# A two-layer ReLU²/cosine network behind linear attention: 1024 tokens take half of their directly computed weight blocks as a third seven-product slot

## The chip, the cores and the metric

One core of a Trainium2 chip runs the whole program. The metric is the device time of one execution in microseconds. In the traces PE is the matrix engine (TensorE), PEld its loading of weights, DVE VectorE, ACT ScalarE, POOL GpSimd, SP SyncE; SP and POOL issue the DMAs, each from a queue that it works through in order.

## The reference

Linear attention with a norm, then two layers of the same shape; 4608 tokens, 512 wide, 2048 hidden. The layers' weights come as 64-bit floats, the rest as 32-bit.

```
kv  = einsum('bhsd,bhse->bhde', k, v)
out = einsum('bhsd,bhde->bhse', q, kv);  x = out / rms(out) * g_norm   # as 4608 x 512
h = x @ w_in;   x = relu(h)**2 @ w_out                                   # first layer
h = x @ w_in2;  out = (h * cos(h)) @ w_out2                              # second layer
```

## The kernel before

**Numbers.** Each 32-bit operand is split into a high half of reduced width and a low half, the rest (`h` on ACT, `l` on DVE), and a product is three matmuls: high-high, high-low, low-high. The 64-bit weights are taken apart into words and made into 32-bit floats on DVE and ACT (`words` L107, `value` L121).

**Stage one** (`run_chunks` L815) works in chunks (t, f): token tile t (nine of 512 tokens) and weight block f. A weight block is 128 of the 2048 hidden columns; the first layer's 16 blocks are shared out, 0 to 7 to stage one (`NH` = 8), 8 to 15 to the slots. A chunk is `layer_in` (12 matmuls of 512 columns into one bank, L374), `act_relu2` (relu, square, halves, L388) and, two chunks later, `layer_out` (12 matmuls into four accumulators, L411). After a tile's last block `evict` (L401) writes the accumulators to `p_d`. Attention runs in between, in the first 49 chunks (`nAtt`). After chunk 49 the square is DVE's work (L396), before it ACT's (L394). There are 72 chunks.

**The slots** (`run_slots` L843) are for the other half of the first layer and for the whole second layer. A slot (m, t, q) is layer m, a tile of 2 x ht tokens (`TILES` L56, ht 512 or 384) and a group q of 4 weight blocks; every product of two 2 x 2 block matrices is made of seven block products instead of eight. A slot has 84 matmuls of ht columns for the first product (`first_product` L499, banks FA and FB) and, in the first layer, 84 of ht columns for the second (`second_product` L629, banks SA and SB); in the second layer the second product's matmuls are 256 columns wide. Combinations of blocks are needed on both sides: `x_block` (L456) makes those of the inputs for a tile's first slot, `s_block` (L590) those of the hidden values (a subtraction for four of the seven, a high half on ACT at L618, a low half on DVE at L619), `add` (L531) and `keep` sum the first product, `drain_product` (L657) adds the second product to the tile's sums (L670). A tile's last slot writes the sums to `y_d`, from which the second layer reads. The first layer has 5 tiles x 2 groups = 10 slots, the second 5 x 4 = 20. First products run ahead of second ones by 1.25 slots (`LAG2`), so PE's time from the first slot's start to slot position 1.25 holds first products only; from there both alternate matmul by matmul.

**Conversion of weights for the slots.** `load_w` (L129) brings a block pair, `conv_steps` (L165) turns it into seven combinations and their halves (four sums or differences at L175, a high half on ACT at L192, a low half on DVE at L194 in two parts of 3 and 4 blocks) and writes them to `wi_d` (first product's weights) or `ws_d` (second product's); `load_wi` and `load_ws` (L485, L490) read them back, 512 KB for each block product. Kinds "pair" and "seven" (512 wide) run in stage one from `w_stream`; kind "pairs" (1024 wide) runs in the slots from `late_stream` (L740), 7 items, for the second layer's first product. Its buffer for the raw words is single (`bufs=1` in `run_slots`' pools), so a load waits until the item before has been stored.

**What sets the order.** Everything that isn't a matmul is a job with a position, in chunks or, after `nA0`, in slots; jobs are sorted by it and emitted between matmuls, and a scheduler then fixes each engine's order, which the engine works through in order. Two lines place what the change touches:

```
w_stream.place(w_at, 0.5, range(2 * NH - NRAW, 2 * NH - NRAW + 2))
late_stream.place([pos(n) for n in (0.95, 2.5, 3.25, 4.5, 6.4, 8.3, 11.3)], 0, lead=0.5)
```

An item of `late_stream` at position n is converted in six steps from n to n + 0.4; the next one is loaded 0.5 ahead of its own position, but not before n + 0.62.

## Time and profile before

| what | value |
|---|---|
| median of 3 runs | 1561.06 us (1559.02 to 1561.68) |
| the profiled execution | 1560.63 us |
| its span | 1558.8 us |
| busy, share of the span | PE 98%, DVE 83%, ACT 69%, POOL 7% |
| TensorE clock granted | full in every slice of the page |
| HBM traffic | 427 MB, 274 GB/s |
| stage one | to 494.86 us |
| the slots | from 494.86 us |

Part 2 of the page cuts the span into 40 slices of 39 us: the first two are the ones in which PE has idle time, and DVE's digits are highest in stage one's second half and in the first slots. Part 4 (the chain that ended last) is PE for 87%. Windows give an engine's busy time for a stretch; a wait is the idle time of an engine before an instruction, put down to what came last.

### The profile page before, as it was taken

To read this page: it belongs to the slowest core of one execution; us is meant where nothing else is said; L and a number is where in the kernel's file an instruction comes from. 1 tells how busy PE (TensorE), PEld (TensorE's weight loads), DVE (VectorE), ACT (ScalarE), POOL (GpSimd) and SP (SyncE) were. 2 spreads that over 40 slices of the span, in tenths; PEclk is the share of its full clock that TensorE was granted. 3 is DMA by queue.
4 is the path that set the end of the run, shared out by engine and by line. 5 is a ranking of instruction groups with operands and counts; after the bars stand their busy time and mean duration, and the time that the engine had idled before them with its cause. 6 is when DMAs were issued, how large, how long until landed. Compare 5 with 4: busy or idle time off the path is not lost.

```text
span 1558.8 us, 24668 instructions
## 1 busy us (share of the span) xinstructions
PE 1533.3 (98%) x9104; PEld 1345.9 (86%) x9104; DVE 1294.2 (83%) x1743; ACT 1077.1 (69%) x1529; POOL 109.8 (7%) x173
## 2 busy tenths in 40 slices
...
GB/s 337 270 149 244 276 283 275 222 214 214 206 226 298 325 253 367 299 380 267 364 339 372 265 281 255 249 285 215 254 247 284 215 247 273 298 326 292 301 311 171
DMA packets 222295, 426.71 MB, mean 274 GB/s; under 512 B 18016, under 2 KB 138080, under 8 KB 222176
## 3 DMA queue, kind: packets, MB, share of 16 engines
...
q10 hardware_dynamic: 160, 0.00, 0.0%
HBM read 317.72 MB, written 81.79 MB: 256 GB/s over the span
## 4 chain that ended last, share of the span: by engine, by line
PE 87%; DVE 5%; DMA 3%; ACT 2%; issue 2%; SPq 0%; POOL 0%; DVEq 0%; ACTq 0%; POOLq 0%
PE FB L509 16%; PE FA L509 16%; PE SA L642 16%; PE SB L642 15%; PE acc L420 11%; PE l L383 9%; PE o L383 1%; PE ss L383 1%; DMA xraw<-x_d 1%; DMA sum<-part 1%; PE o L259 1%; DMA ws_d<-raw 1%; DMA kvld<-in_kv 1%; DVE gl L619 1%; PE l L259 1%
## 5 line engine op out<-in xcount | busy, mean ns | idle before, releaser
L509 PE MATMUL FB<-xh,wi 128*128 128x512 f32 (+1 forms) x840 | 301.4, 370 | 0.0
L509 PE MATMUL FA<-xh,wi 128*128 128x512 f32 (+1 forms) x840 | 301.4, 370 | 0.0
L642 PE MATMUL SB<-ws,gh 128*128 128x256 f32 x1008 | 233.0, 280 | 0.6 <-ACT part L667 0.6
L642 PE MATMUL SA<-ws,gh 128*128 128x256 f32 x1008 | 233.2, 280 | 0.0
L642 PEld LDWEIGHTS SA<-ws,gh 128*128 128x128 f32 x1008 | 183.7, 188 | 12.8 <-issue 0.5
L642 PEld LDWEIGHTS SB<-ws,gh 128*128 128x128 f32 x1008 | 183.3, 188 | 12.6 <-ACT part L667 0.8
L509 PEld LDWEIGHTS FB<-xh,wi 128*128 128x128 f32 x840 | 157.2, 188 | 9.6
L509 PEld LDWEIGHTS FA<-xh,wi 128*128 128x128 f32 x840 | 157.1, 188 | 9.0
L642 PE MATMUL SB<-ws,gl 128*128 128x256 f32 x504 | 141.2, 280 | 0.3 <-DVE gl L619 0.3
L642 PE MATMUL SA<-ws,gl 128*128 128x256 f32 x504 | 141.2, 280 | 0.1
L619 DVE TENSOR_TENSOR gl<-y,gh 128x1024 fp32r<-128x1024 f32 (+1 forms) x98 | 109.5, 1118 | 36.7 <-ACT gh L618 36.7
L668 POOL DMA_DIRECT2D sum<-part x54 | 47.2, 874 | 1136.2 <-DMA wi_d<-raw 530.6
L579 DVE SCALAR_TENSOR_TENSOR y<-y,h 128x1024 f32<-128x1024 f32 (+1 forms) x79 | 88.2, 1117 | 46.1 <-ACT y L575 45.8
L561 ACT ACTIVATE y<-h,zerob 128x1024 int32<-128x1024 f32 (+1 forms) x79 | 84.1, 1065 | 48.7 <-DVE h L535 48.1
L420 PE MATMUL acc<-gh,wh 128*128 128x512 f32 x288 | 113.5, 396 | 1.6 <-ACT og L304 1.6
L420 PE MATMUL acc<-gl,wh 128*128 128x512 f32 x288 | 112.9, 392 | 0.0
L420 PE MATMUL acc<-gh,wl 128*128 128x512 f32 x288 | 112.6, 391 | 0.0
L509 PE MATMUL FA<-xl,wi 128*128 128x512 f32 (+1 forms) x300 | 111.0, 370 | 0.0
L509 PE MATMUL FB<-xl,wi 128*128 128x512 f32 (+1 forms) x300 | 110.9, 370 | 0.0
L571 ACT ACTIVATE y<-y 128x1024 f32<-128x1024 f32 (+1 forms) x79 | 77.2, 978 | 36.5 <-DVE y L565 36.4
L642 PE MATMUL SA<-gh,ws 128*128 128x512 f32 (+1 forms) x280 | 100.8, 369 | 0.9 <-ACT wh L192 0.7
L642 PE MATMUL SB<-gh,ws 128*128 128x512 f32 (+1 forms) x280 | 100.5, 369 | 0.9 <-DMA ws<-ws_d 0.9
...
## 6 DMA issues: line engine op xcount, KB each, us to landing
wi<-wi_d SPq DMA_DIRECT2D x210, 512.0 KB, 6.5
ws<-ws_d SPq DMA_DIRECT2D x210, 512.0 KB, 5.9
sum<-part POOLq DMA_DIRECT2D x33, 512.0 KB, 7.3
kvld<-in_kv SPq DMA_DIRECT2D x32, 512.0 KB, 7.8
...
p_d<-ev SPq DMA_DIRECT2D x18, 512.0 KB, 3.9
raw<-in_wA SPq DMA_DIRECT2D x16, 512.0 KB, 7.3
```

What stands on the lines that cost most here:

```text
L259: nc.tensor.matmul(kv_ps[b][r, p, r], t[:n, 0, head], t[:n, 1, head], start=(c == 0 and p == 0), stop=(c == NSC - 1), skip_group_check=True,)
L383: nc.tensor.matmul(ps, a[:, 0, cs], m[:], start=(c == 0 and k == 0), stop=(c == NKC - 1 and k == 2))
L420: nc.tensor.matmul(o, a[:, cs], m[:], start=(f == 0 and n == 0), stop=(f == NH - 1 and n == 2), skip_group_check=True)
L509: nc.tensor.matmul(ps[:, pp, :], a, b, start=(n == 0 and (i in (0, 2) or i == 1 and not seeded(k))), stop=(n == 5), skip_group_check=True,)
L561: nc.scalar.activation(out=y.bitcast(I32), in_=hs[k, b], func=AF.Identity, bias=zerob)
L571: nc.scalar.activation(out=y, in_=y, func=AF.Sin, scale=math.pi)
L579: nc.vector.scalar_tensor_tensor(out=y, in0=y, scalar=-2.0 * math.pi, in1=hs.pop((k, b)), op0=ALU.add, op1=ALU.mult)
L619: nc.vector.tensor_tensor(out=l, in0=src, in1=as32(h), op=ALU.subtract)
L642: nc.tensor.matmul(ps[:, b, :], lhs, rhs, start=(n == 0 and (m == 0 or b % 2 == 0) and i in (0, 1, 2)), stop=(n == 5), skip_group_check=True,)
L668: nc.gpsimd.dma_start(out=e, in_=part, accum_op=ALU.add)
```

## The change

- Tokens 3584 to 4607 (stage one's tiles 7 and 8) do only blocks 0 to 3 in stage one: 64 chunks instead of 72. Their blocks 4 to 7 become a third group, q = -1, of the first layer's last tile: 11 slots in the first layer, 31 in all.
- The tiles are cut anew (512, 384, 384, 512, 512) and the slots take them in the order 0, 3, 1, 2, 4 in the first layer and 0, 3, 4, 1, 2 in the second: two 512, two 384, one 512, and then three 512, two 384.
- The third group needs weights 4 to 7 in the form of the slots. Stage one has them as 32-bit floats; POOL stores those to `wf_d` (8 stores of 256 KB), and four new items of `late_stream`, "pairs32" and "sevens32", load them and do the combinations and halves without taking words apart.
- Block pair 0 of the second layer moves from `w_stream` (two "pair" items at the end of stage one) to `late_stream`, which now has 12 items at new positions.
- The square after the relu is ACT's in all chunks.

```
@@ -53,7 +53,10 @@
     TOK = 512
     NTILE = NT // TOK
     BIG = 1024
-    TILES = [(0, 512), (BIG, 512), (2 * BIG, 512), (3 * BIG, 384), (3 * BIG + 768, 384)]
+    TILES = [(0, 512), (BIG, 384), (BIG + 768, 384), (NT - 2 * BIG, 512), (NT - BIG, 512)]
+    TILE_ORDER = ((0, 3, 1, 2, 4), (0, 3, 4, 1, 2))
+    SHORT = (4,)
+    FS = [NH // 2 if any(TILES[u][0] <= t * TOK < TILES[u][0] + 2 * TILES[u][1] for u in SHORT) else NH for t in range(NTILE)]
     assert sum(2 * ht for _, ht in TILES) == NT
     LAG = 2
     NDIRECT = 2
...
@@ -75,11 +78,18 @@
     p_d = [dram.tile([P, NKC, TOK], F32, name=f"p_d{t}") for t in range(NTILE)]
     y_d = [dram.tile([P, 2, NKC, ht], F32, name=f"y_d{t0}") for t0, ht in TILES]
     first_pair = (NP, 0)
-    groups_of = [range(NP // 2), range(NP)]
+    all_groups = [range(-1, NP // 2), range(NP)]
     wi_d = {
-        (m, q): dram.tile([P, NPR, 2, 2, 2, P], F32, name=f"wi_d{m}_{q}") for m in range(2) for q in groups_of[m]
+        (m, q): dram.tile([P, NPR, 2, 2, 2, P], F32, name=f"wi_d{m}_{q % NP}") for m in range(2) for q in all_groups[m]
     }
-    ws_d = {k: dram.tile([P, NPR, 2, 2, 2, P], F32, name=f"ws_d{k[0]}_{k[1]}") for k in wi_d}
+    ws_d = {k: dram.tile([P, NPR, 2, 2, 2, P], F32, name=f"ws_d{k[0]}_{k[1] % NP}") for k in wi_d}
+    wf_d = {f: dram.tile([P, 2, DM], F32, name=f"wf_d{f}") for f in range(NH // 2, NH)}
+
+    def groups_of(m, t):
+        if m:
+            return (0, 1, 2, 3)
+        return (0, 1, -1) if t in SHORT else (0, 1)
+
     banks = {"o": ["o", "acc0", "acc2"], "ss": ["ss", "acc1", "acc3"], "l": ["l0", "l1"]}
 
     pools = {}
...
@@ -143,6 +153,17 @@
             for df, dst in ((0, raw[:, 1:3]), (1, raw[:, 0::3])):
                 src = (wA, wB)[m][2 * f + df, :, 0, :].rearrange("p (k n) -> p k n", n=4 * P)
                 nc.sync.dma_start(out=dst.rearrange("p k n two -> p k (n two)"), in_=src)
+        elif kind in ("pairs32", "sevens32"):
+            raw = pools["raw"].tile([P, 4, 2 * P, 2], U32, tag="raw", name="raw")
+            a = as32(raw.rearrange("p a n two -> p (a n two)")).rearrange("p (o n) -> p o n", n=2 * P)
+            lo, hi = (wf_d[2 * f + df][:, int(kind == "sevens32"), :].rearrange("p (k n) -> p k n", n=2 * P) for df in range(2))
+            if kind == "pairs32":
+                nc.sync.dma_start(out=a[:, 1:3], in_=lo)
+                nc.sync.dma_start(out=a[:, 0:4:3], in_=hi)
+            else:
+                nc.sync.dma_start(out=a[:, 1], in_=lo[:, 0])
+                nc.sync.dma_start(out=a[:, 0], in_=lo[:, 1])
+                nc.sync.dma_start(out=a[:, 2:4], in_=hi)
         else:
             if i:
                 raw = x_p.tile([P, DM, 2], U32, tag="xr", name="raw", bufs=2)
...
@@ -164,13 +185,16 @@
 
     def conv_steps(kind, m, f, i):
         raw = raws.pop((kind, m, f, i))
-        if kind in ("pair", "seven", "pairs"):
-            n = 2 * P if kind == "pairs" else P
-            w, e = words(raw, [P, 4, n])
+        if kind != "one":
+            n = P if kind in ("pair", "seven") else 2 * P
+            fp64 = kind in ("pair", "seven", "pairs")
+            if fp64:
+                w, e = words(raw, [P, 4, n])
             yield
 
             a = as32(raw.rearrange("p a n two -> p (a n two)")).rearrange("p (o n) -> p o n", n=n)
-            value(raw, a[:, 0:4], w, e)
+            if fp64:
+                value(raw, a[:, 0:4], w, e)
             for o, x, op, y in ((4, 0, ALU.add, 3), (5, 4, ALU.subtract, 1), (6, 1, ALU.subtract, 0), (7, 2, ALU.subtract, 5)):
                 nc.vector.tensor_tensor(out=a[:, o], in0=a[:, x], in1=a[:, y], op=op)
             where = [p for p in ("c", "x") if p in pools]
...
@@ -204,6 +228,8 @@
         h, l = (x[:, i, :] for x in wts[m, f])
         nc.scalar.copy(out=h, in_=wf)
         nc.vector.tensor_tensor(out=l, in0=wf, in1=as32(h), op=ALU.subtract)
+        if f in wf_d:
+            nc.gpsimd.dma_start(out=wf_d[f][:, i, :], in_=wf)
 
 
     xraw = {}
...
@@ -385,15 +411,12 @@
                     )
         return pss
 
-    def act_relu2(ps, busy):
+    def act_relu2(ps):
         r, g = (temp([P, TOK], F32, n) for n in "rg")
         h = g_p.tile([P, TOK], F32R, tag="gh", name="gh")
         l = g_p.tile([P, TOK], F32R, tag="gl", name="gl")
         nc.scalar.activation(out=r, in_=ps, func=AF.Relu)
-        if busy:
-            nc.scalar.activation(out=g, in_=r, func=AF.Square)
-        else:
-            nc.vector.scalar_tensor_tensor(out=g, in0=ps, scalar=0.0, in1=r, op0=ALU.max, op1=ALU.mult)
+        nc.scalar.activation(out=g, in_=r, func=AF.Square)
         nc.scalar.copy(out=h, in_=g)
         nc.vector.tensor_tensor(out=l, in0=g, in1=as32(h[:]), op=ALU.subtract)
         return h, l
...
@@ -418,13 +441,13 @@
             cs = slice(i * P, (i + 1) * P)
             for n, (a, m) in enumerate(((wh, gh), (wh, gl), (wl, gh))):
                 nc.tensor.matmul(
-                    o, a[:, cs], m[:], start=(f == 0 and n == 0), stop=(f == NH - 1 and n == 2), skip_group_check=True
+                    o, a[:, cs], m[:], start=(f == 0 and n == 0), stop=(f == FS[t] - 1 and n == 2), skip_group_check=True
                 )
-            if f == NH - 1:
+            if f == FS[t] - 1:
                 evict(t, i, o)
 
 
-    slots = [(m, t, q) for m in range(2) for t in range(len(TILES)) for q in groups_of[m]]
+    slots = [(m, t, q) for m in range(2) for t in TILE_ORDER[m] for q in groups_of(m, t)]
     ORDER = (0, 1, 3, 2, 5, 4, 6)
     W_OF = (0, 1, 3, 4, 6, 5, 2)
     BLOCKS = {(0, 0): 2, (1, 1): 5, (0, 1): 6, (1, 0): 7}
...
@@ -679,8 +702,8 @@
 
 
 
-    chunks = [(t, f) for t in range(NTILE) for f in range(NH)]
-    nA0 = NTILE * NH
+    chunks = [(t, f) for t in range(NTILE) for f in range(FS[t])]
+    nA0 = len(chunks)
     nAtt = 49
     LAG2 = 1.25
     jobs = []
...
@@ -731,14 +754,18 @@
             10,
             nAtt + 1,
         ),
-        (pairs_in(0, range(NP, 2 * NP)) + pairs_in(1, range(1)), nAtt + 1, nA0 - 5),
+        (pairs_in(0, range(NP, 2 * NP)), nAtt + 1, nA0 - 5),
     ):
         w_items += new
         w_at += [n0 + (n1 - n0) / len(new) * k for k in range(len(new))]
     w_stream = Stream(load_w, conv_w, w_items)
     w_stream.place(w_at, 0.5, range(2 * NH - NRAW, 2 * NH - NRAW + 2))
-    late_stream = Stream(load_w, conv_w, [("pairs", 1, p, 0) for p in range(1, 2 * NP)])
-    late_stream.place([pos(n) for n in (0.95, 2.5, 3.25, 4.5, 6.4, 8.3, 11.3)], 0, lead=0.5)
+    late_stream = Stream(load_w, conv_w, (
+        [("pairs", 1, p, 0) for p in range(NP)]
+        + [(kind, 0, p, 0) for kind in ("pairs32", "sevens32") for p in range(NP // 2, NP)]
+        + [("pairs", 1, p, 0) for p in range(NP, 2 * NP)]
+    ))
+    late_stream.place([pos(n) for n in (0.55, 1.25, 2.5, 3.2, 4.5, 5.2, 6.5, 7.2, 8.5, 9.3, 11.5, 12.3)], 0, lead=0.5)
 
     kv_stream = Stream(load_kv, kv_mm, [(b, c) for b in range(B) for c in range(NSC)])
     starts = [(-13, 1), (-3, 0.8)] + [(-3 + 7 * (b - 1), 7 / (2 * NKC)) for b in range(2, B)]
...
```

The rest of the diff renames along (`groups_of` as a function, `chunks.index((t, 0))` for a tile's first chunk).

In the orders below, line numbers of the changed kernel are higher by 10 to 27: L175 becomes L199, L192 L216, L194 L218, L464 L487, L483 L506, L509 L532, L539 L562, L595 L618, L619 L642, L642 L665, L670 L693; `words` and `value` stand at L121 to L135.

DVE in slot 1, before, from the subtraction for the third second product (`t<-h,t`) to the low half of the fourth (`gl<-h,gh`):

```order
L595 TENSOR_TENSOR t<-h,t 128x1024
L464 TENSOR_TENSOR xt<-xraw 128x1024
L670 TENSOR_TENSOR sum<-SA,sum 128x1024
L619 TENSOR_TENSOR gl<-t,gh 128x1024
L483 TENSOR_TENSOR xraw<-xraw,xh 128x1024
L670 TENSOR_TENSOR sum<-SB,sum 128x1024
L619 TENSOR_TENSOR gl<-h,gh 128x1024
```

The same place now. The row ahead of these is the first of the conversion at 1.25 (`e<-raw`), the only row of this piece that needs the raw load:

```order
L123 TENSOR_SCALAR w<-raw 128x1024
L487 TENSOR_TENSOR xt<-xraw 128x1024
L126 SCALAR_TENSOR_TENSOR w<-raw,w 128x1024
L642 TENSOR_TENSOR gl<-t,gh 128x1024
L132 SCALAR_TENSOR_TENSOR e<-raw,e 128x1024
L506 TENSOR_TENSOR xraw<-xraw,xh 128x1024
L135 SCALAR_TENSOR_TENSOR raw<-w,e 128x1024
L693 TENSOR_TENSOR sum<-SA,sum 128x1024
L199 TENSOR_TENSOR raw<-raw 128x256 x3
L506 TENSOR_TENSOR xl<-xraw,xh 128x1024
L199 TENSOR_TENSOR raw<-raw 128x256
L642 TENSOR_TENSOR gl<-h,gh 128x1024
```

The conversion's `words`, `value` and combinations (L123 to L135, L199) now stand between the low halves of the third and the fourth second product; before, the last part of the conversion at 0.95 stood ahead of this piece.

SP's queue at the same place, before: the store of the conversion at 0.95 (`wi_d<-raw`) and the load for the next.

```order
L196 DMA wi_d_0_92<-wh 128x4x256
L197 DMA wi_d_0_92<-raw 896x1x256
L488 DMA wi<-wi_d_0_90 128x1024
L493 DMA ws<-ws_d_0_96 128x1024
L488 DMA wi<-wi_d_0_90 128x1024
L493 DMA ws<-ws_d_1_97 128x1024
L488 DMA wi<-wi_d_0_90 128x1024
L145 DMA raw<-in_wB 128x1024
L145 DMA raw<-in_wB 128x2x512
```

Now: the stores of the conversion at 0.55 (all three), and the load for the next.

```order
L220 DMA wi_d_0_93<-wh 128x3x256
L220 DMA wi_d_0_93<-wh 128x4x256
L221 DMA wi_d_0_93<-raw 896x1x256
L473 DMA xraw<-x_d_73 128x2x384
L473 DMA xraw<-x_d_74 128x2x128
L511 DMA wi<-wi_d_1_92 128x1024
L155 DMA raw<-in_wB 128x1024
L155 DMA raw<-in_wB 128x2x512
L473 DMA xraw<-x_d_72 128x2x320
L473 DMA xraw<-x_d_73 128x2x192
```

Two parts of the next tile's input and one weight load stand between store and load, where three weight loads of one kind and two of the other stood; the other half of the next tile's input (`xraw<-x_d`) stands behind the load.

PE in slot 3, now, where the conversions at 2.5 and 3.2 follow closely (L532 is the first product, L665 the second):

```order
L665 MATMUL SB<-gh,ws 128x512
L532 MATMUL FA<-xh,wi 128x512
L532 MATMUL FA<-xl,wi 128x512
L532 MATMUL FA<-xh,wi 128x512 x2
L532 MATMUL FA<-xl,wi 128x512
L532 MATMUL FA<-xh,wi 128x512 x2
L532 MATMUL FA<-xl,wi 128x512
L532 MATMUL FA<-xh,wi 128x512 x2
L532 MATMUL FA<-xl,wi 128x512
L532 MATMUL FA<-xh,wi 128x512
L665 MATMUL SA<-gh,ws 128x512
L665 MATMUL SA<-gl,ws 128x512
```

Twelve first-product matmuls stand in a row ahead of the third second product; before, first and second alternated there.

## Rows read from the trace of the kernel before

**Rows 1.** Page, part 1: busy time of two engines over the span.

```profile
span 1558.8 us, 24668 instructions
PE 1533.3 (98%) x9104; PEld 1345.9 (86%) x9104; DVE 1294.2 (83%) x1743; ACT 1077.1 (69%) x1529; POOL 109.8 (7%) x173
```

**Rows 2.** Chain that ended last, in order of time: start, length, piece.

```profile
486.70 8.16 PE acc L420 x36
494.86 2.72 PE FA L509 x12
```

**Rows 3.** Waits of PE from 490 us to the end: total, times, longest.

```profile
PE SB L642 <- DMA ws<-ws_d: 0.9, 1, 0.9
PE SA L642 <- ACT wh L192: 0.7, 1, 0.7
PE SB L642 <- ACT part L667: 0.6, 1, 0.6
```

**Rows 4.** Windows: end of stage one, then four stretches of the slots.

```profile
core 0: us, PE busy (x) PEld busy (x) DVE busy (x) ACT busy (x) POOL busy (x), PEclk, DMA share, GB/s
360.00:495.00 135.00, 135.00 (x597) 111.59 (x596) 101.26 (x188) 59.29 (x92) 1.06 (x2) 1.00 0.71 228
494.86:518.60 23.74, 23.74 (x106) 19.65 (x106) 16.53 (x19) 17.02 (x18) 0.00 (x0) 1.00 0.94 332
518.60:585.30 66.70, 66.70 (x296) 55.24 (x295) 65.22 (x61) 43.15 (x44) 0.00 (x0) 1.00 0.86 283
585.30:661.50 76.20, 75.53 (x333) 62.23 (x333) 72.54 (x72) 47.57 (x48) 0.00 (x0) 1.00 0.91 332
661.50:870.00 208.50, 207.41 (x1065) 189.80 (x1065) 185.06 (x193) 127.83 (x149) 0.00 (x0) 1.00 0.91 337
```

**Rows 5.** DVE and ACT groups by form: count, busy us, mean ns.

```profile
L396 DVE SCALAR_TENSOR_TENSOR g<-l,r 128x512 f32<-128x512 f32 x12 | 8.3, 689 | 11.2 <-ACT r L392 11.2
L398 DVE TENSOR_TENSOR gl<-g,gh 128x512 fp32r<-128x512 f32 x72 | 49.5, 687 | 6.2 <-ACT gh L397 6.0
L116 DVE SCALAR_TENSOR_TENSOR w<-raw,w 128x1024 uint32<-128x1024 uint32 x7 | 8.5, 1220 | 0.1
L175 DVE TENSOR_TENSOR raw<-raw 128x256 f32<-128x256 f32 x28 | 10.5, 418 | 0.1
L194 DVE TENSOR_TENSOR raw<-raw,wh 128x1024 fp32r<-128x1024 f32 x7 | 8.5, 1216 | 0.0
L194 DVE TENSOR_TENSOR raw<-raw,wh 128x768 fp32r<-128x768 f32 x7 | 6.7, 953 | 4.1 <-ACT wh L192 3.8
L394 ACT ACTIVATE g<-r 128x512 f32<-128x512 f32 x49 | 31.1, 634 | 0.6
```

**Rows 6.** DVE in order of time, slots 1 to 3: start, length, instruction.

```profile
508.56 1.23 DVE L539 TENSOR_TENSOR h<-FA,m 128x1024 f32<-128x1024 f32 x1 [1.10 <-PE FA L509]
...
524.18 1.21 DVE L595 TENSOR_TENSOR t<-h,t 128x1024 f32<-128x1024 f32 x1
525.31 1.22 DVE L464 TENSOR_TENSOR xt<-xraw 128x1024 f32<-128x1024 f32 x1
...
527.58 1.21 DVE L619 TENSOR_TENSOR gl<-t,gh 128x1024 fp32r<-128x1024 f32 x1
...
533.25 1.22 DVE L619 TENSOR_TENSOR gl<-h,gh 128x1024 fp32r<-128x1024 f32 x1
...
593.41 0.69 DVE L111 TENSOR_SCALAR e<-raw 128x1024 uint32<-128x1024 uint32 x1 [1.38 <-DMA raw<-in_wB]
```

**Rows 7.** Page, part 6: DMA issues, KB each, us to landing.

```profile
raw<-in_wB SPq DMA_DIRECT2D x14, 512.0 KB, 7.6
wi_d<-raw SPq DMA_DIRECT2D x7, 896.0 KB, 5.6
```

**Rows 8.** SP's DMA queue in order of time, slot 1.

```profile
523.16 0.52 SPq L197 DMA_DIRECT2D wi_d<-raw  x1
531.34 1.59 SPq L145 DMA_DIRECT2D raw<-in_wB  x2
```

77 lines of the change are left out of this document (51 added, 26 removed).

## The prediction

> **What bounds the kernel now.** I read four views in this order. Part 1 of the page [rows 1] has PE busy for 98% of the span and DVE for 83%. The page counts matmuls that overlap, so busy time alone doesn't say that PE is the limit. The chain that ended last does [rows 2]: stage one ends with 36 matmuls in 8.16 us, the slots start at 494.86 us with 12 in 2.72 us, and nothing lies between. A 512-column matmul costs 8.16 / 36 = 2.72 / 12 = 0.2267 us of PE's time, on either side of that line. From 490 us on PE waits hardly at all: the three longest waits are 0.9, 0.7 and 0.6 us [rows 3]. So the slots run at PE's pace, and a matmul that is taken out is worth its 0.2267 us, as long as the next engine keeps up. The next engine is DVE. The windows [rows 4] show where it has room: 101.26 us busy of 135 at the end of stage one, 65.22 of 66.70 (98%) in slots 1 and 2, 72.54 of 76.20 (95%) in slots 3 and 4, 185.06 of 208.50 (89%) in the rest of the first layer. In slots 1 and 2 DVE has nothing to give.
>
> **The profiled execution** took 1560.63 us, 0.43 below the median of 1561.06. I sum against 1560.63 and add the 0.43 at the end.
>
> **Removed from stage one.** Eight chunks (tokens of tiles 7 and 8, weight blocks 4 to 7). A chunk is 12 matmuls in and 12 out: 8 x 24 = 192, or 192 x 0.2267 = 43.5 us of PE [rows 2]. DVE loses 8 of the low halves of 0.687 us and all 23 squares of 0.689 us that it did after chunk 49 [rows 5] (the row has the 12 that read from one bank), 21 us in all. The squares go to ACT at 634 ns [rows 5], which is busy 59.29 us of 135 there [rows 4], so the way from PSUM to the low half gets no longer, and layer_out needs it two chunks (10.9 us) later. I cost that at nothing; its cover is ACT's free half.
>
> **Added: one slot of 512-token blocks.** 84 matmuls of the first product and 84 of the second, 168 x 0.2267 = 38.1 us of PE. **PE's balance is 24 matmuls, -5.44 us**, and it holds whatever the tile order is, because there are as many 512 and 384 tiles as before. DVE gets 20 operations of 128x1024 for that slot (2 sums, 11 for the second product's operands, 7 additions to the sums). They start 1.13 us apart [rows 6], so 23 us beside 38 us of PE: this slot has more room than any other.
>
> **Added: four conversions from float32** (pairs32, sevens32). Each is 4 x 0.418 + 0.953 + 1.216 = 3.8 us of DVE [rows 5]. They sit in the slots of the 384 tiles, where one full conversion sat for each tile before: by the same rows a full one is 3.8 + 3 x 1.22 + 2 x about 0.69 = 8.9 us, so two short ones (7.6) are no heavier. They cost nothing as long as the 11% of free DVE stays. The new slot's 14 loads of 512 KB (7.3 MB) and the 2.3 MB that each short conversion reads and writes are 16.5 MB beside 38 us of added PE work. The four slot windows moved 122 MB in 375 us [rows 4], 326 GB/s; with both added it is 336, 3% more, and I cost that at nothing too. The 8 stores of wf_d (256 KB each, POOL's queue) fall into the first chunks and nothing waits for them before slot 4; behind them on POOL's queue are only x_d stores, read five chunks later.
>
> **Moved: one more full conversion into slots 0 to 2.** Block pair 0 of the second layer leaves stage one. Before, slots 0 to 2 held a conversion at 0.95 and one at 2.5; now 0.55, 1.25 and 2.5. That is 8.9 us more for an engine that is 98% busy in slots 1 and 2. Slot 0 has 7 us free (16.53 busy of 23.74), which the first of them fills. The second one decides. I follow it on the clock of before (all of it is 43.5 us earlier now):
> - The first conversion's last subtraction now stands right behind the sum of 508.56 [rows 6], so it ends near 511, and its store follows at once; before, the store left at 523.16 [rows 8].
> - The raw buffer is single. The store lands 5.6 us later, and the next load then takes 7.6 us [rows 7] after about 1 us of issue: 511 + 0.5 + 5.6 + 0.9 + 7.6 = 525.6. Before, SP issued that load 8 us after the store [rows 8] with half a slot to spare; now 0.08 slot is left.
> - DVE reaches the conversion's first row after the subtraction that ended at 525.4 [rows 6], now some 2 us sooner, so it waits about 2 us for the load. Before, it met such a wait once, 1.38 us [rows 6].
> - The low half that ended at 528.8 [rows 6] then ends near 530; PE wants it at 518.6 + 2 x 5.44 = 529.5 plus one matmul, so this one is level. The next stood 5.7 us behind it (527.58 to 533.25); six long and four short rows now lie between, 8.2 us. It ends near 538.4, with PE asking at 535.2: about 3 us late. The order of PE has a few first-product matmuls put ahead there, which hide about 1 us.
>
> DVE's backlog lasts until slot 3, where the pair at 2.5 and 3.2 is closer by 0.05 slot (1.9 us) than before; there a run of 12 first-product matmuls ahead of the second product covers 2.7 us. I take 2 us of new stall in slot 1 and 1 us in slot 3, and that 1 us of the old stalls [rows 3] goes with the order that made them: **+2 us net**. Lower bound: -2.2 us (the three waits of rows 3 all vanish). Upper bound: all of the 8.9 us, if nothing hides any of it. I stay near the lower part because DVE's free 5% and 11% come right after.
>
> Behind the load of slot 1, SP's queue holds the operand loads of the next tile; held for about 5 us, they still land some 7 us before DVE's operands need them.
>
> Sum: 1560.63 - 5.44 + 2.0 = 1557.2; with 0.43, **1557.6 us**.
>
> [...] The row says 7.6 us for the landing of a raw load in this kernel's traffic [rows 7]. [...]
>
> **Rivals.**
> 1. *Nothing stalls.* DVE's work of slots 0 to 2 fits after all, and the old waits go too. For it: PE's order is made to step around late operands, and in slots 3 and 4 PE lost only 76.20 - 75.53 = 0.7 us with DVE 95% busy [rows 4]. Against it: 98%. Time: 1561.06 - 5.44 - (0 to 2.2) = 1553.4 to 1555.6.
> 2. *The stall eats the gain.* The store or the load of slot 1 lands at the far end of what a raw load is seen to need, and the backlog is paid again at 3.2: 4 to 8 us of new stall, 1559.6 to 1563.6. For it: each us by which the load is late moves every later row of DVE. Against it: PE's runs ahead.
> 3. *SP's queue blocks, and it gets slower.* The load waits in SP's queue for the single raw buffer, and all that stands behind it waits too: weights, next tile's operands. Before, the pairs of conversions that follow closely were one (2.5 and 3.25); now there are five (0.55/1.25, 2.5/3.2, 4.5/5.2, 6.5/7.2, 8.5/9.3). With 2 us of PE each, as in slot 1, and 1.5 us more in slots 1 and 3, that is 13 us against 5.44, or 1569; it turns slower than before from 1.1 us each, and slower than 0.2% from 1.7 us each. Against it: in the 384 tiles the f32 loads are half as large and DVE has 11% to spare, so I expect under 0.5 us there. Time: 1564.2 to 1569.
> That the change doesn't do what it says is excluded by the orders: PE has 24 wide matmuls less.
>
> **How the numbers follow.** A measurement here can tell about 0.2%, 3.1 us, from no change: faster means under 1557.9, slower over 1564.2. My forecast, net stall of 0.5 to 4 us (1556.1 to 1559.6), has 0.55, with 0.33 of it under 1557.9; rival 1 has 0.17, rival 2 0.18, rival 3 0.10. Faster 0.33 + 0.17 = 0.50; slower 0.10; same 0.40. The range leaves out the lower third of rival 1 and rival 3: 1554.0 to 1564.0.
>
> **What would show it.** In the new profile the slots should begin near 451 us; DVE should wait about 2 us for the raw load at the second wide conversion (near 481 us) and PE one to three us for the low half of the fourth second product there. Slot 10, the third of the last tile, should have no PE wait. If PE waits under 1 us in slots 1 to 4, rival 1 is right; if SP's queue shows long waits for wi_d stores and PE waits for ws or wi loads, rival 3. The forecast is wrong if stage one ends later than 453 us: then the denser conversions at its end, or the POOL stores at its start, cost what I put at nothing.

## The result and the profile after

The changed kernel takes 1575.93 us (median of 4 runs, 1573.66 to 1577.36) where the kernel before took 1561.09 on the same chip: ratio 1.0096, 95% interval 1.0079 to 1.0114. It is **14.8 us slower**; I had forecast 3.5 us faster, with a range up to 1564.0. The profiled execution took 1575.98 us. Part 1 of its page, against [rows 1]:

```profile
span 1574.1 us, 24732 instructions
...
PE 1535.6 (98%) x9080; PEld 1344.6 (85%) x9080; DVE 1309.8 (83%) x1747; ACT 1102.3 (70%) x1554; POOL 114.5 (7%) x181
```

PE has 24 matmuls less than before, as the order said, and yet 2.3 us more busy time: some matmuls took longer. Busy shares tell nothing else, so I cut the span at four matmuls that exist in both kernels (start times in the trace, by line) and set against it what each piece would take if PE were its only limit:

| piece, us | before | after | by PE alone | lost |
|---|---|---|---|---|
| start to the last attention matmul | 355.7 | 357.6 | 355.7 | 1.9 |
| to the first matmul of the slots | 139.0 | 99.6 | 139.0 - 43.5 = 95.5 | 4.1 |
| to the second layer's first second product | 371.3 | 423.9 | 371.3 + 38.1 = 409.4 | 14.5 |
| to the last matmul | 688.1 | 688.0 | 688.1 | 0 |

1.9 + 4.1 + 14.5 lost and 5.4 gained is 15.1 of the 15.35 us between the two profiled executions. The second layer runs as before. The 1.9 us are taken up under e4_stores; nearly all of the rest lies in three places, and at each a conversion of weights stands among the rows.

**End of stage one.** VectorE in order of time (the brackets hold the idle time in front of the row and what ended it):

```profile
414.48 0.43 DVE L121 TENSOR_SCALAR e<-raw 128x512 uint32<-128x512 uint32 x1 [3.37 <-DMA raw<-in_wA]
...
429.56 0.43 DVE L121 TENSOR_SCALAR e<-raw 128x512 uint32<-128x512 uint32 x1 [3.87 <-DMA raw<-in_wA]
```

VectorE stands at the first row of a conversion whose load has not landed. Behind it in the queue are the copies and low halves that PE wants, and PE's list of waits from 358 to 457 us has them, 2.6 of the 4.1 us:

```profile
PE acc L443 <- DVE ev L431: 1.7, 1, 1.7
PE acc L443 <- ACT gh L420: 0.9, 1, 0.9
```

**Slot 1.** SP's queue, where the store of the first conversion and the load of the second answer to [rows 8]:

```profile
475.06 0.53 SPq L221 DMA_DIRECT2D wi_d<-raw  x1
...
480.26 1.49 SPq L155 DMA_DIRECT2D raw<-in_wB  x2
```

Then VectorE, ScalarE and PE, each in order of time:

```profile
480.24 1.23 DVE L642 TENSOR_TENSOR gl<-h,gh 128x1024 fp32r<-128x1024 f32 x1 [4.07 <-ACT gh L641]
...
488.29 0.69 DVE L121 TENSOR_SCALAR e<-raw 128x1024 uint32<-128x1024 uint32 x1 [1.03 <-DMA raw<-in_wB]
...
491.77 1.22 DVE L642 TENSOR_TENSOR gl<-t,gh 128x1024 fp32r<-128x1024 f32 x1
...
495.18 1.22 DVE L135 SCALAR_TENSOR_TENSOR raw<-w,e 128x1024 f32<-128x1024 uint32 x1
496.32 1.22 DVE L693 TENSOR_TENSOR sum<-SA,sum 128x1024 f32<-128x1024 f32 x1
```

```profile
490.08 1.03 ACT L641 CAST gh<-t 128x1024 fp32r<-128x1024 f32 x1
...
496.44 0.83 ACT L216 CAST wh<-raw 128x768 fp32r<-128x768 f32 x1 [3.42 <-DVE raw L135]
...
498.09 1.04 ACT L641 CAST gh<-h 128x1024 fp32r<-128x1024 f32 x1
```

```profile
493.01 0.39 PE L532 MATMUL FA<-xh,wi 128*128 128x512 f32 x1
497.64 0.77 PE L665 MATMUL SA<-gh,ws 128*128 128x512 f32 x1 [4.24 <-ACT wh L216]
```

The load landed 8.0 us after its issue and VectorE waited 1.03 us for it: that much was foreseen. PE stood 4.24 us. The view names ScalarE's `wh`, but that row had ended at 497.27, 0.37 us before PE went on, and PE needed nothing more of ScalarE: both halves of its operand, `gh<-t` and `gl<-t`, were done by 493.0 (the `gh` of 498.09 starts when PE is running again). PE's queue holds one row of line 665 in that time, a wait for semaphores, which began at 489.2 and took 8402 ns, to 497.58:

```profile
L665 PEldq EVENT_SEMAPHORE  x1: 8402/8402/8402, 489.2 to 489.2; - x1
```

What ended just ahead of that is VectorE's `sum<-SA,sum` (496.32 + 1.22 = 497.54). The third second product is accumulated in bank SA on top of the first (it is product 3 of the seven, and in `second_product` only products 0, 1 and 2 start a bank anew), so it can't begin before VectorE has added the first one to the tile's sums. That addition now stands in VectorE's queue behind the conversion's `w`, `e` and `raw<-w,e`, where in the kernel before it stood ahead of the low half `gl<-t`. And then (windows of 2 us, in the columns of [rows 4]):

```profile
494.00:496.00 2.00, 0.00 (x0) 0.00 (x0) 2.00 (x3) 0.00 (x0) 0.00 (x0) 1.00 1.00 408
496.00:498.00 2.00, 0.36 (x1) 0.39 (x2) 2.00 (x4) 1.56 (x2) 0.00 (x0) 0.59 0.37 152
498.00:500.00 2.00, 2.00 (x6) 1.52 (x6) 2.00 (x5) 1.13 (x2) 0.00 (x0) 0.50 0.97 301
500.00:502.00 2.00, 2.00 (x6) 1.56 (x5) 2.00 (x4) 1.96 (x3) 0.00 (x0) 0.50 0.97 379
502.00:504.00 2.00, 2.00 (x8) 1.58 (x7) 2.00 (x3) 0.95 (x2) 0.00 (x0) 0.70 0.85 307
504.00:506.00 2.00, 2.00 (x10) 1.66 (x9) 2.00 (x3) 1.06 (x1) 0.00 (x0) 1.00 0.25 91
```

The granted clock falls to 0.50 during the wait, and when PE goes on it stays there until about 503 us. Six matmuls start in 2 us instead of nine. From 497.64 on that costs 0.2 + 1.0 + 1.0 + 0.6 = 2.8 us more, so this stall is worth **7.0 us**, not 4.2. In the kernel before the granted clock was 1.00 in all four stretches of the slots in [rows 4].

**The 384 tiles.** ScalarE, VectorE and PE near 706 us, then windows of all engines:

```profile
700.62 0.84 ACT L216 CAST wh<-raw 128x768 fp32r<-128x768 f32 x1 [5.40 <-DMA raw<-wf_d]
...
707.29 0.83 ACT L641 CAST gh<-t 128x768 fp32r<-128x768 f32 x1 [4.25 <-DVE t L618]
```

```profile
704.30 0.96 DVE L693 TENSOR_TENSOR sum<-SB,sum 128x768 f32<-128x768 f32 x1 [1.82 <-PE SB L665]
705.18 1.21 DVE L199 TENSOR_TENSOR raw<-raw 128x256 f32<-128x256 f32 x3
706.31 0.95 DVE L618 TENSOR_TENSOR t<-h,t 128x768 f32<-128x768 f32 x1
```

```profile
708.18 0.69 PE L665 MATMUL SA<-gh,ws 128*128 128x384 f32 x1 [2.35 <-ACT gh L641]
...
710.52 0.69 PE L665 MATMUL SA<-gl,ws 128*128 128x384 f32 x1 [1.34 <-DVE gl L642]
```

```profile
680.00:700.00 20.00, 20.00 (x117) 20.00 (x117) 14.12 (x16) 9.16 (x12) 0.00 (x0) 1.00 1.05 388
...
708.00:710.00 2.00, 1.01 (x2) 0.50 (x2) 2.00 (x3) 2.00 (x4) 0.00 (x0) 0.50 1.03 386
710.00:712.00 2.00, 1.48 (x5) 1.48 (x6) 2.00 (x3) 2.00 (x4) 0.00 (x0) 0.50 1.11 397
712.00:714.00 2.00, 2.00 (x8) 2.00 (x7) 2.00 (x3) 1.82 (x3) 0.00 (x0) 0.50 1.03 416
```

Here ScalarE stands 5.40 us for the load of a short conversion (`raw<-wf_d`) while the DMA engines are full (share 1.03 and over, near 400 GB/s). But that wait ended at 700.62, and the chain that ends PE's wait of 2.35 us holds no load: VectorE waits for PE's own product in SB, adds it, does three combinations of the short conversion and then `t`, and ScalarE casts `gh` from it. From 680 to 700 us, with the DMA engines as full, PE waited for nothing. The two waits are 3.7 us, the half clock behind them some 2.6, together 6.3. Slot 1 and this place are 13.3 of the 14.5 us. Another 1.1 us (PE 38.88 busy of 40) lies near 570 us, in slot 3.

### The profile page after: what moved, and what is told of

It reads as the page before. It is cut to its first block, busy times and chain, and to the rows that moved or that the text cites. A ratio compares the mean times of both kernels' runs of the same rounds, so it can differ in the third digit from the quotient of the medians.

```text
span 1574.1 us, 24732 instructions
## 1 busy us (share of the span) xinstructions
PE 1535.6 (98%) x9080; PEld 1344.6 (85%) x9080; DVE 1309.8 (83%) x1747; ACT 1102.3 (70%) x1554; POOL 114.5 (7%) x181
## 4 chain that ended last, share of the span: by engine, by line
PE 74%; DMA 10%; DVE 9%; issue 3%; ACT 3%; SPq 0%; POOL 0%; DVEq 0%; ACTq 0%; POOLq 0%
PE SA L665 15%; PE SB L665 14%; PE FB L532 14%; PE FA L532 14%; PE acc L443 7%; PE l L409 6%; DMA wi_d<-raw 2%; DMA wi<-wi_d 1%; DMA raw<-in_wA 1%; DMA ws_d<-raw 1%; DMA raw<-in_wB 1%; DVE gl L642 1%; DVE sum L693 1%; DVE raw L218 1%; DMA xraw<-x_d 1%
## 5 line engine op out<-in xcount | busy, mean ns | idle before, releaser
L532 PE MATMUL FA<-xh,wi 128*128 128x512 f32 (+1 forms) x872 | 313.0, 371 | 1.0 <-ACT h L571 0.6
L532 PE MATMUL FB<-xh,wi 128*128 128x512 f32 (+1 forms) x864 | 311.7, 372 | 0.1
L665 PE MATMUL SA<-ws,gh 128*128 128x256 f32 x1008 | 232.9, 280 | 0.2 <-ACT part L690 0.2
L665 PE MATMUL SB<-ws,gh 128*128 128x256 f32 x1008 | 232.5, 280 | 0.0
L665 PEld LDWEIGHTS SB<-ws,gh 128*128 128x128 f32 x1008 | 183.3, 188 | 12.0
L665 PEld LDWEIGHTS SA<-ws,gh 128*128 128x128 f32 x1008 | 183.2, 188 | 12.1 <-ACT part L690 0.4
L532 PEld LDWEIGHTS FA<-xh,wi 128*128 128x128 f32 x872 | 163.5, 188 | 13.3 <-ACT h L571 1.0
L532 PEld LDWEIGHTS FB<-xh,wi 128*128 128x128 f32 x864 | 162.5, 189 | 11.5 <-ACT u L552 0.5
L665 PE MATMUL SA<-ws,gl 128*128 128x256 f32 x504 | 141.3, 280 | 0.3 <-DVE gl L642 0.3
L665 PE MATMUL SB<-ws,gl 128*128 128x256 f32 x504 | 141.3, 280 | 0.1
L642 DVE TENSOR_TENSOR gl<-y,gh 128x1024 fp32r<-128x1024 f32 (+1 forms) x98 | 109.5, 1117 | 35.7 <-ACT gh L641 35.5
L665 PE MATMUL SA<-gh,ws 128*128 128x512 f32 (+1 forms) x312 | 114.5, 379 | 6.6 <-ACT wh L216 4.2
L532 PE MATMUL FA<-xl,wi 128*128 128x512 f32 (+1 forms) x312 | 115.9, 371 | 0.0
L532 PE MATMUL FB<-xl,wi 128*128 128x512 f32 (+1 forms) x308 | 114.6, 372 | 0.0
L665 PE MATMUL SB<-gh,ws 128*128 128x512 f32 (+1 forms) x304 | 108.4, 370 | 0.0
L443 PE MATMUL acc<-gh,wh 128*128 128x512 f32 x256 | 100.6, 398 | 4.2 <-DVE ev L431 1.7
L693 DVE TENSOR_TENSOR sum<-SA,sum 128x1024 f32<-128x1024 f32 (+1 forms) x78 | 87.4, 1121 | 19.2 <-PE SA L665 14.9
L443 PE MATMUL acc<-gl,wh 128*128 128x512 f32 x256 | 100.6, 393 | 0.3 <-DVE gl L421 0.3
```

What stands on the lines that cost most here:

```text
L443: nc.tensor.matmul(o, a[:, cs], m[:], start=(f == 0 and n == 0), stop=(f == FS[t] - 1 and n == 2), skip_group_check=True)
L532: nc.tensor.matmul(ps[:, pp, :], a, b, start=(n == 0 and (i in (0, 2) or i == 1 and not seeded(k))), stop=(n == 5), skip_group_check=True,)
L642: nc.vector.tensor_tensor(out=l, in0=src, in1=as32(h), op=ALU.subtract)
L665: nc.tensor.matmul(ps[:, b, :], lhs, rhs, start=(n == 0 and (m == 0 or b % 2 == 0) and i in (0, 1, 2)), stop=(n == 5), skip_group_check=True,)
L693: nc.vector.tensor_tensor(out=e, in0=ps, in1=e, op=ALU.add)
```

## The experiments

Seventeen kernels. The last two columns are the second and third piece of the table above; by PE alone they are 95.5 and 409.4 us with the third slot, 139.0 and 371.3 without.

| kernel | median, us | ratio to before, 95% | end of stage one | slots, first layer |
|---|---|---|---|---|
| e4_stores | 1560.99 | 1.0009, 1.0000 to 1.0018 | 138.9 | 370.6 |
| e5_squares | 1559.77 | 0.9998, 0.9990 to 1.0007 | 138.9 | 370.4 |
| e9_order | 1563.23 | 1.0023, 1.0013 to 1.0032 | 139.0 | 373.8 |
| e6_slot | 1559.49 | 0.9998, 0.9990 to 1.0007 | 100.3 | 409.9 |
| e1_spacing | 1576.84 | 1.0108, 1.0091 to 1.0125 | 95.3 | 428.5 |
| e2_interleave | 1572.80 | 1.0085, 1.0070 to 1.0100 | 99.4 | 419.9 |
| e3_spread | 1581.76 | 1.0147, 1.0132 to 1.0162 | 99.3 | 422.8 |
| e10_spaced | 1569.56 | 1.0059, 1.0045 to 1.0072 | 101.5 | 416.2 |
| e11_early | 1585.80 | 1.0163, 1.0149 to 1.0177 | 99.9 | 432.9 |
| e8_dose14 | 1571.42 | 1.0074, 1.0061 to 1.0087 | 139.0 | 382.2 |
| e12_traffic | 1574.19 | 1.0089, 1.0074 to 1.0104 | 100.6 | 420.0 |
| e13_nostore | 1565.89 | 1.0035, 1.0023 to 1.0048 | 99.7 | 413.4 |
| e14_second_raw | 1569.34 | 1.0068, 1.0054 to 1.0082 | 100.3 | 417.0 |
| e15_third_raw | 1564.71 | 1.0033, 1.0021 to 1.0044 | 98.1 | 416.0 |
| e16_both_spaced | 1563.08 | 1.0018, 1.0009 to 1.0027 | 95.3 | 415.2 |
| e17_one_in_384 | 1559.22 | 0.9999, 0.9990 to 1.0007 | 95.4 | 412.1 |
| e18_short_first | 1562.03 | 1.0010, 1.0001 to 1.0019 | 95.4 | 415.0 |

### The parts alone

**e4_stores**: the kernel before, with

```diff
+    wf_d = {f: dram.tile([P, 2, DM], F32, name=f"wf_d{f}") for f in range(NH // 2, NH)}
...
+        if f in wf_d:
+            nc.gpsimd.dma_start(out=wf_d[f][:, i, :], in_=wf)
```

> The kernel before with one part of the change alone: the eight stores of weight blocks 4 to 7 as 32-bit floats by POOL in the first chunks, which nothing reads. Theory 'stores at the start': PE was 1.6 us behind by 100 us in the changed kernel and 1.9 by 350; the stores alone give +1.5 to 2 us, 1562.5 to 1563. Rival: the delay comes from the other tile numbers or order, the stores cost nothing: 1561.

Measured +1.65 us, with an interval that begins at 0. In its profile nearly all of it lies before the last attention matmul (357.6 us, as in the changed kernel). Over all kernels of this study that mark is at 355.0 to 356.0 us in the five without these stores (mean 355.4) and at 355.7 to 358.1 in the fourteen with them (mean 356.7), one profile of each: about 1.3 us, which I had put at nothing.

**e5_squares**: the kernel before, with

```diff
-            gs[chunks[n]] = act_relu2(ps, n < nAtt)
+            gs[chunks[n]] = act_relu2(ps, True)
```

> The kernel before with the last 23 squares of stage one by ScalarE instead of VectorE, nothing else. My theory (cost nothing: ScalarE has the room and layer_out needs the low half two chunks later): 1559.3 us as before, within 0.2% (3 us), stage one as long as before (139.0 us from the last attention matmul to the first slot matmul). Rival (the squares on ScalarE are part of the 4.1 us that the end of stage one came late): stage one's end 1 to 4 us longer and the time 1560.3 to 1563.3.

Level. The squares cost nothing, as I had them.

**e9_order**: the kernel before, with

```diff
-    TILES = [(0, 512), (BIG, 512), (2 * BIG, 512), (3 * BIG, 384), (3 * BIG + 768, 384)]
+    TILES = [(0, 512), (BIG, 384), (BIG + 768, 384), (NT - 2 * BIG, 512), (NT - BIG, 512)]
+    TILE_ORDER = ((0, 3, 1, 2, 4), (0, 3, 4, 1, 2))
```

> The kernel before with the tiles cut and ordered as in the changed one (512, 384, 384, 512, 512; first layer 0, 3, 1, 2, 4, second layer 0, 3, 4, 1, 2), nothing else: no third slot, stage one and its conversions as before. In the first layer a tile of 512 now follows the two of 384, in the second the 384s are last as before. My theory (the order costs nothing by itself, as there are as many tiles of each size and the conversions stay where they are): 1559.3, within 0.2%; the slots of the first layer take 371 us. Rival (the traffic and the operands of the 384 tiles in the middle are a cost of the order, part of the stall near 706 us): the slots take 373 to 377 us, the time is 1561.5 to 1565, and PE waits 1 us or more between 650 and 725 us.

Slots 2.5 us longer, so the rival's number, but not at its place: the largest wait is 1.8 us at 769 us. The view names a conversion's cast (`SB <- ACT wh`), but what ended at the same time, at 769.1, is VectorE's `sum<-SB,sum`, behind a conversion's rows as in slot 1. The same order loses 0.5 us in e6_slot, where the conversions stand otherwise. So the order costs what it does by where the conversions then stand.

**e6_slot**: the changed kernel, with

```diff
-            nc.gpsimd.dma_start(out=wf_d[f][:, i, :], in_=wf)
...
-        + [(kind, 0, p, 0) for kind in ("pairs32", "sevens32") for p in range(NP // 2, NP)]
...
+    late_stream = Stream(load_w, conv_w, [("pairs", 1, p, 0) for p in range(2 * NP)])
+    late_stream.place([pos(n) for n in (0.95, 2.5, 4, 5.5, 7, 8.5, 10, 11.3)], 0, lead=0.5)
...
-        nc.sync.dma_start(out=as32(w[:]), in_=wi_d[m, q][:, W_OF[i]])
+        nc.sync.dma_start(out=as32(w[:]), in_=wi_d[m, max(q, 0)][:, W_OF[i]])
...
```

> The changed kernel without the eight stores of wf_d and without the four conversions from float32: the third slot of the last tile multiplies with the weights of group 0 instead (the weights of blocks 4 to 7 are left out there, so the output isn't the reference's); the eight full conversions of the second layer stand 1.3 to 1.6 slots apart (0.95, 2.5, 4, 5.5, 7, 8.5, 10, 11.3). It keeps the third slot, the tile order, the squares, stage one's dense spacing. My theory (the balance of 24 matmuls is worth its 5.4 us where nothing stalls; the end of stage one loses 4.1 us from the spacing; the stores 1.7 to 1.9): the last attention matmul near 355.7 us, stage one's end still about 99.5 us after it, the slots of the first layer about 409.4 to 412 us instead of 423.9, no wait of PE over 2 us in them and the granted clock 1.00 throughout: 1559.3 - 5.4 + 4.1 + (0 to 2.6) = 1558 to 1560.6. Rival (the third slot or the tile order itself, not the conversions, makes the stalls of the slots): the slots of the first layer take 418 us or more and the time is 1565 or more.

As expected in every piece: slots 409.9 us where PE alone needs 409.4. A third slot, its loads and the tile order run at PE's pace, so the balance of -5.44 us is real. The end of stage one still loses 4.8 us here. What the changed kernel loses in the slots comes with the conversions.

### Where the conversions stand

**e1_spacing**: the changed kernel, with

```diff
-        (pairs_in(0, range(NP, 2 * NP)), nAtt + 1, nA0 - 5),
+        (pairs_in(0, range(NP, 2 * NP)), nAtt + 1, nA0 - 0.5),
```

> The changed kernel with the eight conversions at the end of stage one spread over chunks 50 to 63.5 instead of 50 to 59 (one each 1.69 chunks, before: 1.70). Theory 'late raw load': DVE stood 3.4 and 3.9 us in front of raw loads there and PE lost 3.5 us between chunk 49 and the first slot; with the old spacing the waits go, the slots begin near 453.5 us instead of 456.7, and the time falls by about 3 us to 1573. Rival 'traffic': the transfers of that stretch (304 GB/s against 251) are what delays PE; the same bytes in the same stretch leave the time at 1576.

Stage one's end comes out at 95.3 us, all 4.1 us back. But its last conversion now runs into the one at slot 0.55, and the first slots give it back: PE waits 3.4 us for `u` near 464 us, and the clock falls there (0.50 from 468 to 470 us); another 4.1 us for `u` at 501 us stand in the place of slot 1's wait. The time is 17.5 us over the kernel before, no better than the changed kernel.

**e2_interleave**: the changed kernel, full and short conversions in turn at the same twelve positions.

```diff
-        [("pairs", 1, p, 0) for p in range(NP)]
-        + [(kind, 0, p, 0) for kind in ("pairs32", "sevens32") for p in range(NP // 2, NP)]
+        [
+            item
+            for p, short in enumerate((kind, 0, p, 0) for kind in ("pairs32", "sevens32") for p in range(NP // 2, NP))
+            for item in (("pairs", 1, p, 0), short)
+        ]
```

> The changed kernel with the items of late_stream in another order at the same positions: a full conversion and a short one in turn, so that no two full ones lie in slots 0 to 1 or in slots 2 to 3. Theory 'DVE backlog, then the clock': the PE wait of 4.2 us at 493.4 us and the stretch at half clock after it go, worth about 7 us; the full conversions that now lie in the 384 tiles bring 0.5 MB more each there, so the stall at 706 us stays or grows: 1568 to 1572. Rival 'traffic': the same bytes, more of them in the stretch that is already at 400 GB/s, 1576 or slower.

Slot 1's stall is gone (PE's longest wait there is 0.3 us), but full conversions in the 384 tiles make longer waits there: 2.2 us for `wi`, 2.2 for `h`, 1.7 for `gl`. Of slot 1's 7.0 us only 4.0 are left as a gain in the slots, and the time is 13.5 us over the kernel before.

**e3_spread**: two short ones early, two late.

```diff
-        [("pairs", 1, p, 0) for p in range(NP)]
-        + [(kind, 0, p, 0) for kind in ("pairs32", "sevens32") for p in range(NP // 2, NP)]
+        [("pairs", 1, 0, 0), ("pairs32", 0, 2, 0), ("pairs", 1, 1, 0), ("pairs32", 0, 3, 0)]
+        + [("pairs", 1, 2, 0), ("pairs", 1, 3, 0), ("sevens32", 0, 2, 0), ("sevens32", 0, 3, 0)]
-    late_stream.place([pos(n) for n in (0.55, 1.25, 2.5, 3.2, 4.5, 5.2, 6.5, 7.2, 8.5, 9.3, 11.5, 12.3)], 0, lead=0.5)
+    late_stream.place([pos(n) for n in (0.55, 1.25, 2.5, 3.2, 4.5, 6.5, 8.5, 9.2, 9.9, 11.4, 12.1, 12.8)], 0, lead=0.5)
```

> The changed kernel with the items of late_stream reordered and spread: the two 384 tiles get one full conversion each, as before the change, and the sevens32 items move to the last 512 tile. Theory 'DVE backlog, then the clock' for the first stall and 'transfers at 400 GB/s' for the second: both stalls (4.2 and 3.7 us) and both half-clock stretches (about 2.8 and 2.7 us) go, -13 us, 1562 to 1564. If only the backlog counts and not the traffic of the 384 tiles, the stall at 706 us stays: 1569. If the positions count for nothing: 1576.

The 384 tiles have no wait over 1 us, and a new stall costs nearly as much as both old ones: 8.9 us and half clock behind it (0.50 from 800 to 804 us). VectorE, ScalarE and PE, each in order of time:

```profile
792.14 0.69 DVE L121 TENSOR_SCALAR e<-raw 128x1024 uint32<-128x1024 uint32 x1
```

```profile
797.16 0.83 ACT L216 CAST wh<-raw 128x768 fp32r<-128x768 f32 x1 [3.15 <-DVE raw L135]
...
798.81 1.03 ACT L641 CAST gh<-h 128x1024 fp32r<-128x1024 f32 x1
```

```profile
799.90 0.80 PE L665 MATMUL SB<-gh,ws 128*128 128x512 f32 x1 [8.94 <-ACT gh L641]
```

With 8.5, 9.2 and 9.9 close together, `gh` stood behind a conversion's cast in ScalarE's queue. No load was late there: the raw load had landed at 781.0, 11 us ahead of VectorE's first row of it. The second layer loses 7.3 us more in this kernel, with a wait of 3.0 us at 925 us; three conversions stand there now (11.4 to 12.8) instead of two. **e10_spaced** (order f s f s f f s f s f f f, f full and s short) and **e11_early** are two more placements:

```diff
-    late_stream.place([pos(n) for n in (0.55, 1.25, 2.5, 3.2, 4.5, 5.2, 6.5, 7.2, 8.5, 9.3, 11.5, 12.3)], 0, lead=0.5)
+    late_stream.place([pos(n) for n in (0.55, 1.25, 2.5, 3.2, 4.2, 5.7, 7.2, 8.5, 9.3, 10.3, 11.5, 12.3)], 0, lead=0.5)
```

> The changed kernel with the conversions placed anew, all of its work kept: stage one's eight last conversions run to 2.5 chunks before its end instead of 5; in the slots full (f) and short (s) conversions in the order f s f s f f s f s f f f at 0.55, 1.25, 2.5, 3.2, 4.2, 5.7, 7.2, 8.5, 9.3, 10.3, 11.5, 12.3, so that only three instead of four stand in the 384 tiles (slots 4 to 7), 1.5 slots apart. My theory (the 14 us that the slots lost come from where conversions stand, not from their number): stage one ends 95.5 to 97 us after the last attention matmul, the slots of the first layer take 410 to 414 us, no granted clock of 0.5 in them, the time is 1556 to 1561. Rival (twelve conversions are too many for the DMA queues and VectorE in eleven slots wherever they stand): the slots take 417 us or more with at least one wait of PE over 2 us, the time is 1564 or more.

> As e10_spaced, with the order f s f s f f f s f s f f at 0.6, 1.5, 2.5, 3.3, 4.1, 5.6, 7.1, 8.0, 8.7, 9.6, 10.4, 11.4: the 384 tiles hold full conversions alone, as before, and both conversions of the second product's weights stand in the slots of the last tile. My theory: the slots of the first layer take 410 to 416 us; a wait in slots 8 to 10, where five conversions follow 0.7 to 0.9 slots apart, is likelier than in the 384 tiles; 1556 to 1562. Rival (twelve are too many): 417 us or more, 1564 or more.

e10_spaced is the best so far in the slots of those with all of the work (416.2 us, no wait over 1.5, no half clock), neither theory's number. Its stage one is worse, though its conversions stand wider than in the changed kernel: PE waits 3.2 us for the last tokens' `xl`, behind a raw load for which VectorE stood 4.8 us. e11_early missed: waits of 5.2 us at 761 and 3.6 us at 832 us, and behind the second the matmuls of 512 columns start 0.43 us apart (832.67 to 837.37). Spacing alone is no cure, and a late load isn't needed for a stall: before both waits of e11_early the raw load had landed 5 and 8 us ahead of VectorE's first row of it, and what PE wanted stood behind the conversion's rows.

### Traffic or rows

**e12_traffic** keeps the short conversions' transfers, **e13_nostore** their rows on the engines:

```diff
+        if kind in ("pairs32", "sevens32"):
...
+            for o, n, x in ((0, 3, 0), (3, 4, 0), (0, 4, 1), (4, 3, 1)):
+                nc.sync.dma_start(out=dst[:, o:o + n, x, :], in_=a[:, :n])
+            return
```

```diff
+                if not kind.endswith("32"):
+                    nc.sync.dma_start(out=dst[:, lo - 1:end - 1, 0, :], in_=as32(h))
+            if not kind.endswith("32"):
+                nc.sync.dma_start(out=dst[:, :, 1, :], in_=as32(l[:, 1:]))
...
```

> The changed kernel, with the rows of the four short conversions on VectorE and ScalarE left out: their loads, and stores of the same 1.8 MB each, stay at their places (the third slot's weights are not computed there). 15 us of VectorE in slots 4 to 7 go, the traffic stays. Theory traffic (the stalls near 706 us come from transfers that arrive late in the 384 tiles): the wait of 2 us or more and the half clock near 706 us stay; the slot 1 stall stays too, as all its rows are those of full conversions; the first layer's slots take 420 us or more, the time is 1571 or more. Theory engines (VectorE's and ScalarE's rows of the short conversions make the waits): no wait over 1.5 us between 640 and 730 us, the slots take 414 to 418 us (4 to 7 of slot 1 stay), the time is 1565 to 1569.

> The changed kernel, with the stores of the four short conversions left out (1.8 of 2.3 MB each; the third slot multiplies with the weights of group 0): every row on VectorE and ScalarE stays at its place, the traffic of the short conversions is a fifth. Theory traffic: no wait over 1.5 us between 640 and 730 us, the slots take 414 to 418 us, the time is 1565 to 1569. Theory engines: the waits and the half clock near 706 us stay, 420 us or more, 1571 or more.

The window from 700 to 720 us, e12_traffic first, then e13_nostore:

```profile
700.00:720.00 20.00, 17.71 (x93) 17.42 (x93) 16.59 (x17) 9.91 (x13) 0.00 (x0) 0.92 1.04 383
```

```profile
700.00:720.00 20.00, 20.00 (x113) 19.38 (x112) 19.37 (x21) 13.23 (x17) 0.00 (x0) 1.00 1.04 413
```

With the transfers and without the rows the 384 tiles still stall (a wait of 2.3 us, clock 0.92 in the mean of the window); with the rows and without the stores they don't: in e13_nostore PE has no wait at all from 640 to 740 us. So the stores are needed for the stall and the rows aren't. How the stores make it is not shown. In the window above e13_nostore moves 413 GB/s and PE waits for nothing. Without the stores the single raw buffer also comes free sooner: in the slots of the changed kernel ScalarE stands 7.1 us for loads of `raw<-wf_d`, in e13_nostore not at all. And the scheduler orders the rows anew for each edit: the wait of e12_traffic is at 716 us and ends with a `sum<-SA,sum` that stands behind VectorE's rows for the next tile's inputs. Slot 1 stalls in both (4.3 and 2.9 us), at the same `sum<-SA,sum`, as full conversions make it.

### The clock

**e8_dose14**: the kernel before, with more work for VectorE at one place.

```diff
+        for _ in range(15 if (k, i) == (4, 4) else 1):
             nc.vector.tensor_tensor(out=l, in0=src, in1=as32(h), op=ALU.subtract)
```

> The kernel before with one low half of the second product (slot 4, its second operand) subtracted 14 times more than needed: 14 x 1.135 = 15.9 us of VectorE at one place near 668 us of a program in which the profile of before shows no wait over 1 us. PE stands 8 to 11 us in front of that operand. Theory A (a stall costs what PE stands, nothing more): the time grows by the wait that the profile shows there and in the rows right behind it, within 1 us, and the granted clock stays 1.00. Theory B (after a stall of this length the granted clock is half for some time, as the profile of the changed kernel shows behind its 4.2 us wait): a stretch of granted clock 0.5 begins within some us of the wait's end, and the time grows by the wait plus half that stretch, 1.7 to 5 us more than by theory A.

The repeats went in among the other rows, so PE stood twice, 2.58 and 5.05 us. Windows of e8_dose14:

```profile
695.00:700.00 5.00, 2.42 (x11) 1.73 (x10) 5.00 (x6) 1.20 (x2) 0.00 (x0) 0.95 1.03 416
700.00:702.00 2.00, 2.00 (x7) 2.00 (x8) 2.00 (x3) 1.85 (x2) 0.00 (x0) 0.50 0.46 188
...
704.00:706.00 2.00, 0.00 (x0) 0.00 (x0) 2.00 (x2) 2.00 (x3) 0.00 (x0) 1.00 0.62 178
...
708.00:710.00 2.00, 1.38 (x3) 1.17 (x4) 2.00 (x3) 0.00 (x0) 0.00 (x0) 0.50 0.00 0
710.00:712.00 2.00, 1.97 (x6) 1.02 (x4) 2.00 (x3) 0.00 (x0) 0.00 (x0) 0.50 0.00 0
```

The waits are 7.6 us; the slots take 10.9 more and the kernel 11.6. Theory B holds: behind each wait the clock is half for a while, and some 3 to 4 us come on top. The DMA engines are idle in the second stretch, so it isn't traffic that slows PE there.

### Loads with more lead

**e14_second_raw**: the changed kernel, with a second raw buffer in the slots and `lead=1` instead of 0.5, so that loads go up to a slot ahead. **e15_third_raw** adds one for stage one (a `raw_pool()` that hands out every third tile from the new pool), **e16_both_spaced** the placement of e10_spaced.

```diff
-                    at(max(n - lead, 0 if k == 0 else positions[k - 1] + steps[-1]), self.advance)
+                    at(max(n - lead, 0 if k < 2 else positions[k - 2] + steps[-1]), self.advance)
...
-    pools["c"] = ctx.enter_context(tc.tile_pool(name="c", bufs=18, side="left", reuse_waits="tile"))
-    pools["raw"] = ctx.enter_context(tc.tile_pool(name="late", bufs=1, side="left", reuse_waits="tile"))
+    pools["c"] = ctx.enter_context(tc.tile_pool(name="c", bufs=16, side="left", reuse_waits="tile"))
+    pools["raw"] = ctx.enter_context(tc.tile_pool(name="late", bufs=2, side="left", reuse_waits="tile"))
```

```diff
+        pools["raw3"] = right("conv3", 1)
+        w_stream.advance()
```

> The changed kernel with two raw buffers for the conversions of the slots instead of one, each load issued up to one slot ahead instead of half; to make room, the pool of the operands keeps 16 tiles instead of 18. Order and positions of the conversions stay, stage one stays. Theory late load (each stall begins with a conversion whose first row stands in VectorE's or ScalarE's queue in front of a load that could not start sooner, because the one buffer was still being stored): VectorE and ScalarE wait under 0.5 us for raw loads in the slots, slot 1's wait falls from 4.2 to 0 to 2.5 us, the one near 706 us goes, the slots take 410 to 417 us, the time is 1561 to 1568. Rival (VectorE simply has too many rows there, or 16 tiles are too few): the loads are on time and PE still waits 3 us or more in slot 1; 419 us or more, 1570 or more.

> As e14_second_raw, and a third raw buffer for the conversions of stage one from chunk 49 on, so that their loads run one conversion further ahead. Theory late load: VectorE no longer stands 3 to 4 us in front of raw loads after 405 us, stage one ends 95.5 to 97.5 us after the last attention matmul, 2 to 4 us less time than e14_second_raw. Rival (the eight conversions at 1.1 chunks apart are too many rows or too much traffic for the end of stage one): still 99 us or more, no more than 1 us less than e14_second_raw.

> As e15_third_raw, with the conversions in the order and at the positions of e10_spaced (full and short in turn, three in the 384 tiles, stage one's last eight up to 2.5 chunks before its end). If late loads are the whole cause, nothing stalls: slots 409.5 to 413 us, stage one's end 95.5 to 97 us, 1556 to 1560, so level with the kernel before or faster. If VectorE's rows or the traffic of twelve conversions bound the slots as well: slots 414 us or more, 1562 or more.

Windows of e14_second_raw, slots 0 to 2, then to 700 us, then the second half of the 384 tiles:

```profile
456.00:560.00 104.00, 103.85 (x457) 85.32 (x457) 100.56 (x103) 70.47 (x73) 0.00 (x0) 1.00 0.94 342
560.00:700.00 140.00, 139.23 (x729) 129.31 (x728) 122.18 (x138) 86.58 (x104) 0.00 (x0) 1.00 0.98 373
700.00:740.00 40.00, 34.66 (x166) 30.49 (x165) 37.77 (x43) 22.27 (x27) 0.00 (x0) 0.96 0.95 370
```

In slots 0 to 2 PE is idle for 0.15 us in 104, with the same rows and VectorE 97% busy. Their order is another one; VectorE in e14_second_raw:

```profile
478.29 1.23 DVE L135 SCALAR_TENSOR_TENSOR raw<-w,e 128x1024 f32<-128x1024 uint32 x1
479.43 1.22 DVE L642 TENSOR_TENSOR gl<-h,gh 128x1024 fp32r<-128x1024 f32 x1
...
488.71 1.21 DVE L693 TENSOR_TENSOR sum<-SA,sum 128x1024 f32<-128x1024 f32 x1
489.85 1.21 DVE L642 TENSOR_TENSOR gl<-t,gh 128x1024 fp32r<-128x1024 f32 x1
```

With the raw words there early, the conversion's first five rows fill the time in which VectorE had stood idle ahead of `gl<-h,gh` (4.07 us in the changed kernel), and `sum<-SA,sum` stands ahead of the low half again. **Slot 1 stalled because the load could come no sooner with a single buffer.** VectorE's wait for it, 1.03 us, was the small part; the large part were the rows that could only follow it. Not tested is another order with the one buffer, with `sum<-SA,sum` ahead of these rows: PE's product in SA was done at 487.1.

After 700 us 5.3 us are still lost. The two longest waits, 2.5 and 1.6 us, end with a `sum<-SA,sum` again, the longer one behind the rows of a conversion whose load was on time; a third, 0.8 us, is for `wi`. So the time (1569.34) lies between the two theories, and the rival's too many rows are part of what is left. The third buffer in stage one is worth another 4.6 us, and 2.2 us of its end; VectorE still stood once for a load there, 3.3 us. With the wider placement (e16_both_spaced) stage one ends at 95.3 us, as by PE alone, and the slots take 415.2, the number of its second theory; three of its four waits of 1 us or more lie from 700 to 725 us.

**e17_one_in_384** and **e18_short_first**: as e16_both_spaced, with the conversions moved out of the 384 tiles.

```diff
-    late_stream.place([pos(n) for n in (0.55, 1.25, 2.5, 3.2, 4.2, 5.7, 7.2, 8.5, 9.3, 10.3, 11.5, 12.3)], 0, lead=1)
+    late_stream.place([pos(n) for n in (0.55, 1.25, 2.2, 3.0, 3.8, 5.5, 8.2, 8.9, 9.6, 10.4, 11.5, 12.3)], 0, lead=1)
```

> As e16_both_spaced, with the conversions f s f s f f s f s f f f at 0.55, 1.25, 2.2, 3.0, 3.8, 5.5, 8.2, 8.9, 9.6, 10.4, 11.5, 12.3: one full conversion in the middle of the 384 tiles instead of two and a short one. Theory traffic (what is left of the stalls in e16_both_spaced, some 5.8 us between 580 and 730 us, is transfers that come late where the 384 tiles alone fill the DMA queues): no wait of PE over 1 us between 640 and 740 us, slots 410 to 413 us, 1557.5 to 1561, level with the kernel before. Rival (the last tile's slots, which now hold six conversions from 8.2 to 10.4, stall as in e11_early although the loads have lead): a wait of 2 us or more between 740 and 840 us, slots 416 us or more, 1564 or more.

> As e17_one_in_384, with the order f s f s s f f s f f f f at 0.55, 1.25, 2.2, 2.9, 3.6, 5.2, 7.8, 8.6, 9.4, 10.2, 11.5, 12.3: three short conversions ahead of the 384 tiles, one full one in them, one short one behind. Theory traffic: as e17_one_in_384, 410 to 413 us, 1557.5 to 1561. Rival (VectorE has no room for a third short conversion before slot 4): a wait of 2 us or more between 530 and 640 us, slots 416 us or more, 1564 or more.

PE's waits in e17_one_in_384 from 455 to 880 us, the three longest (total, times, longest):

```profile
PE SA L671 <- DVE gl L648: 1.1, 1, 1.1
PE FA L538 <- ACT FA L571: 1.0, 2, 0.7
PE SB L671 <- ACT xh L511: 0.8, 1, 0.8
```

No half clock, slots 412.1 us, 1559.22 us: 0.8 us under the kernel before on the same chip, which is level, where the changed kernel was 14.8 above; it has all of its work and one buffer more at each of the two places. The numbers of the traffic theory came true, but a conversion that leaves the 384 tiles takes its rows along with its transfers, so this doesn't tell the two apart. The four conversions from 8.2 to 10.4 (not six, as I had written) stall nothing with more lead for their loads; at 8.0, 8.7, 9.6 and 10.4 in e11_early, in the same order and with one buffer, they met the waits of 5.2 and 3.6 us. e18_short_first met one wait of 2.1 us at 788 us and its half clock (0.86 in the mean of 790 to 800 us), and neither theory's place or time. No version beat the kernel before: of the 5.4 us, the profile of e17_one_in_384 loses 1.0 before the last attention matmul, 2.7 in the slots of the first layer and 1.0 in the second layer.

## Why the prediction was wrong

By its own steps:

- **PE's balance, -5.44 us: right.** e6_slot has the slots within 0.5 us of it.
- **Squares at nothing: right** (e5_squares).
- **Slot 1, 2 us of new stall: right place, wrong row, 7.0 us in size.** The raw load landed 31.0 us after the slots began, where I had worked out 30.7, and VectorE waited 1.03 us for it. The step that failed is the one that called the third second product level: I looked for its low half alone, which was indeed level (493.0), and went on to the fourth. PE stood at the third, for `sum<-SA,sum`, which the order printed ahead of the prediction has four rows behind that low half, 4 x 1.13 = 4.5 us. The four first-product matmuls ahead of it hid 0.9 us, about as foreseen, and PE stood 4.24 us. Then the granted clock, which the sum does not have at all, added 2.8.
- **Slot 3, 1 us: right in size**, 1.1; and from 745 us to the end of the first layer, slot 10 with it, PE has no wait, as foreseen.
- **The four short conversions and their traffic at nothing: wrong, 6.3 us.** I counted VectorE's rows, divided 122 MB by 375 us and found 3% more traffic. That average hides the 384 tiles, where the same loads serve three quarters of the columns and the DMA engines are full (share 1.03 to 1.11, 386 to 416 GB/s, from 708 to 714 us). e12_traffic and e13_nostore show that the stall there needs the short conversions' stores; whether through the traffic, the raw buffer that they hold or the order of the rows stays open.
- **Stage one's denser conversions at nothing: wrong, 4.1 us.** The sum has no term for them; they stand in it only as the test at its end. The loads were late, because SP's queue held them until stores had left the raw buffers (15.7 us of such waits for `wi_d` stores, in six pieces, from 358 to 457 us). The kernel before has as much of that, 22.2 us in eight pieces, but with conversions 1.7 chunks apart VectorE stood 0.6 us for the loads there; with 1.1 it stood 10.3. The test that I had named, an end later than 453 us, came true at 457.2.
- **The POOL stores at nothing: wrong by 1.3 us.** That nothing waits for them is true; why they cost anything is not shown.
- **Rival 3** was the nearest: pairs of conversions that follow closely and a single raw buffer. It had 0.10, because I priced its places in the 384 tiles at under 0.5 us each, where VectorE had 11% to spare. VectorE's spare time was no cover there. That its 1569 comes near is luck in part: it has five places of 2 us, and the trace has two stalls, of 4.2 and 3.7 us, and no half clock (2.8 + 2.6 us) or stores in the sum; and PE waited for VectorE's and ScalarE's rows, not for `ws` or `wi` loads.

What the sum lacked is in the views above: the half clock behind a wait of PE (2.8 us in slot 1, some 2.6 in the 384 tiles), and `sum<-SA,sum` behind `raw<-w,e` in VectorE's queue (496.32 behind 495.18).
